# Router logits by a grouped product with a late selector, and another order from the second group's marks to the first gathered rows

## The chip, the cores and the metric

The kernel runs on one core of one Trainium2 chip. The metric is the device time of one execution in microseconds; the median of three runs before the change is 969.06 us (968.68 to 971.01). Engines are named as the profile names them: PE is TensorE (PEld its weight loads), DVE is VectorE, ACT is ScalarE, POOL is GpSimd, SP is the engine that issues most DMAs.

## What is computed

Three layers in a row, all in float32:

```python
# 1. attention: 4 batches, 8 heads, 576 tokens, 64 wide, window of 64 keys
scores = scale * np.matmul(q, k.transpose(0, 1, 3, 2))   # masked outside the window
attn = softmax(scores)
x = np.matmul(attn, v)                                   # -> [2304, 512]
# 2. noisy top-2 router over 8 experts, each 512 -> 1024 -> 512
logits = x @ w_gate
noise_scale = np.log1p(np.exp(x @ w_noise))
noisy_logits = logits + noise_scale * noise
# the two largest per token, softmax over the two
out[mask] += top2_w[mask, k, None] * (np.maximum(x[mask] @ w1[e], 0.0) @ w2[e])
# 3. a dense layer 512 -> 2048 -> 512 with a piecewise quadratic gate
```

The router chooses by the values of the logits, so these are computed in full float32.

## The kernel before, in words

The 2304 tokens are 18 tiles of 128. The attention stage is a pipeline of half-tile steps `u` (0 to 36, `step`, L674); an even step and the odd one after it handle one tile. Everything is issued in program order, and each engine runs its own instructions in that order, so a wait of one instruction holds all behind it on its engine. In an even step stand the scores of the next tile (`A`, L347, products at L355 and L364), the transposes of a finished tile of x (`Ex`, L417: four transposes at L421, a copy by ScalarE at L423), the transposes of a block of probabilities (`C`, L387, copy L389), the row maxima (`top`, L371 on VectorE, scaled on GpSimd at L373) and the exponentials (`soft`, L380 on ScalarE). `Dm` (L392) multiplies by v (L401), normalises on VectorE (L406, L407, L409), issues the store of the tile of x to DRAM (`x_dram`, L412) and moves half a tile of v for the next tile (L414, on GpSimd). Weight chunks for the experts are split into a high and a low part meanwhile (L161 on ScalarE, L162 on VectorE).

The logits of tile i come from `Gm` (L434) in an odd step: four accumulated products (L439; float32 takes two passes each, so eight in the trace) with the transposed tile as weights (128 columns) and 16 columns of router weights moving, into a PSUM bank from a rota of two (`rot`), and a copy to SBUF by VectorE (L442). `wg` in DRAM holds 32 columns a block, of which 16 are zeros.

Tiles are routed in three groups of six (`GROUPS`). When the sixth tile of a group has its logits, `logits` (L667) starts the generator `route` (L488): a chain of small VectorE operations with two ScalarE functions (L500 to L524), the two largest (L528, L531), one-hot rows (L541), their positions by matmuls (L556 to L560), and then twelve marks, two per tile. A mark is a one-hot row on VectorE (`ohr`, L584) and a step row (`ohe`, on VectorE at L591 for odd tiles, on ScalarE at L594 for even ones); its matmul (`place`, L626, at L632) adds it to a table of row numbers in bank 7. `advance` runs the generator in each step, with at most `MARKS` marks: 2 in steps up to 26, 4 from step 27 on; 4 (`TAIL`) behind the attention stage.

When all 24 marks of the first two groups are placed, `early` (L717) runs `finish_ids` (copy of the table L459, four small operations L472 to L475 that give `src_i`) and issues three gathers of rows on GpSimd (L726) for expert 0's first three blocks. `bump` (L606) then corrects the count of expert 0. `xpose` (L739) transposes a gathered block (L748), copies its high part by ScalarE (L751) and its low part by VectorE (L752). The last steps do it like this:

```python
    for u in range(NU + 1):
        step(u)
        ...
        for b in range((0, 1, NA)[max(u - NU + 2, 0)]):
            if ("0a", b) in gat:
                xpose("0a", b, P, Sb[b])
```

The expert stage follows: per chunk a first-layer product (`mm1`, L869; ReLU and split into `h0a` at L877 and L880), and a second-layer product (`mm2`, L935). The logits of the last two tiles, the transposes of the last tile and the third group's chain run in `tail` (L772), a generator of which the loop over the chunks takes one step twice per chunk of expert 0 (`more`):

```python
    def tail():
        logits(NT - 2, NU + 1)
        Ex(NT - 1, NU + 1)
        advance(TAIL)
        yield
        logits(NT - 1, NU + 1)
        while live or oq or pq:
            place()
            advance(TAIL)
            yield
```

## Time and profile before

| | |
|---|---|
| median of 3 runs | 969.06 us |
| profiled execution, its own time | 969.4 us |
| its span, first to last instruction | 967.7 us |
| TensorE busy | 98% of the span |
| VectorE, ScalarE, GpSimd busy | 68%, 46%, 23% |
| mean granted TensorE clock | 0.993 of full speed |

The profile is one execution. Its page gives busy times and groups; the trace behind it can be asked for windows (busy time of each engine in a stretch, with the granted clock), for a timeline in order of time, and for waits (who stood, and what ended it). Times in a timeline are microseconds from the start of the span. Operations that overlap in the pipeline of one engine are merged with their like, so the distance from one start to the next is the better price of a short operation. A releaser in brackets is inferred from semaphores, and where several were waited for it can be another one.

### The profile page before, as it was taken

To read this page: it belongs to the slowest core of one execution; us is meant where nothing else is said; L and a number is where in the kernel's file an instruction comes from. 1 tells how busy PE (TensorE), PEld (TensorE's weight loads), DVE (VectorE), ACT (ScalarE), POOL (GpSimd) and SP (SyncE) were. 2 spreads that over 40 slices of the span, in tenths; PEclk is the share of its full clock that TensorE was granted. 3 is DMA by queue.
4 is the path that set the end of the run, shared out by engine and by line. 5 is a ranking of instruction groups with operands and counts; after the bars stand their busy time and mean duration, and the time that the engine had idled before them with its cause. 6 is when DMAs were issued, how large, how long until landed. Compare 5 with 4: busy or idle time off the path is not lost. (4 is left out here: it accounts for less than half of the span.)

```text
span 967.7 us, 18329 instructions
## 1 busy us (share of the span) xinstructions
PE 944.2 (98%) x6918; PEld 837.0 (86%) x6918; DVE 660.7 (68%) x1377; ACT 446.8 (46%) x921; POOL 218.6 (23%) x269
## 2 busy tenths in 40 slices
PE   8998899999999999999999999999999999999997
PEld 6887789998898988889888888888999899899996
DVE  4689375578997968798442366666766777677664
ACT  6887224356555555555332366344325334442221
POOL 3221113244535434344301020013002201300000
PEclk9999799999999999999999999999999999999999
DMA  8875116557877976967837357584576558556521
GB/s 249 294 236 177 56 45 204 209 195 254 285 253 261 288 250 215 298 218 238 331 118 273 119 197 244 195 302 138 175 261 213 173 174 305 174 164 209 187 95 44
DMA packets 92797, 201.17 MB, mean 208 GB/s; under 512 B 7433, under 2 KB 17929, under 8 KB 92705
## 3 DMA queue, kind: packets, MB, share of 16 engines
q1 hardware_dynamic: 85264, 177.84, 55.4%
q0 software_dynamic: 6144, 19.76, 5.7%
q10 hardware_dynamic: 1296, 2.36, 0.6%
q8 instruction: 55, 0.90, 0.4%
q14 instruction: 38, 0.30, 0.1%
HBM read 159.65 MB, written 40.29 MB: 207 GB/s over the span
## 5 line engine op out<-in xcount | busy, mean ns | idle before, releaser
L935 PE MATMUL bank<-wo,hg 128*128 128x512 f32 x864 | 238.2, 394 | 0.0
L935 PE MATMUL bank<-w,he 128*128 128x512 f32 (+3 forms) x696 | 170.5, 396 | 0.0
L935 PEld LDWEIGHTS bank<-wo,hg 128*128 128x128 f32 x864 | 147.0, 189 | 17.3
L935 PEld LDWEIGHTS bank<-w,he 128*128 128x128 f32 (+3 forms) x696 | 124.7, 184 | 26.7
L869 PE MATMUL bank<-xhie,w 128*128 128x288 f32 (+4 forms) x768 | 120.9, 299 | 1.6 <-DVE he L880 1.5
L869 PEld LDWEIGHTS bank<-xhie,w 128*128 128x128 f32 x768 | 112.0, 188 | 8.6 <-DVE he L880 3.5
L877 ACT ACTIVATE he<-bank 128x288 fp32r<-128x288 f32 (+4 forms) x96 | 40.2, 419 | 149.7 <-PE bank L869 146.1
L162 DVE TENSOR_TENSOR w<-raw,w 128x1024 fp32r<-128x1024 f32 (+1 forms) x71 | 82.0, 1154 | 32.8 <-ACT w L161 32.1
L1188 PEld LDWEIGHTS bank<-xb,wi 128*128 128x128 f32 x576 | 81.6, 191 | 12.2 <-ACT r L887 1.7
L1188 PE MATMUL bank<-xb,wi 128*128 128x256 f32 x576 | 85.9, 285 | 2.4 <-ACT r L887 1.4
L1212 ACT ACTIVATE hg<-cg 128x512 fp32r<-128x512 f32 x64 | 40.3, 629 | 100.5 <-DVE cg L1210 100.5
L1188 PEld LDWEIGHTS bank<-xc,wi 128*128 128x128 f32 x480 | 67.2, 188 | 7.6 <-DVE wg L1173 0.6
L1048 POOL TENSOR_TENSOR y<-y,y 128x512 f32<-128x512 f32 x14 | 19.1, 1362 | 228.2 <-ACT y L1047 228.2
L1188 PE MATMUL bank<-xc,wi 128*128 128x256 f32 x480 | 70.2, 281 | 0.2
L161 ACT ACTIVATE w<-raw 128x1024 fp32r<-128x1024 f32 (+1 forms) x71 | 69.3, 977 | 0.0
L869 PE MATMUL bank<-xloe,w 128*128 128x288 f32 (+4 forms) x384 | 68.1, 299 | 0.0
L880 DVE SCALAR_TENSOR_TENSOR he<-bank,he 128x320 fp32r<-128x320 f32 (+8 forms) x120 | 43.2, 399 | 34.0 <-ACT he L877 33.9
L207 POOL TENSOR_TENSOR td<-rawd 128x512 f32<-128x512 f32 x32 | 33.3, 1040 | 133.5 <-DVE rawd L205 73.7
L1206 ACT ACTIVATE mg<-cg 128x512 f32<-128x512 f32 x64 | 40.0, 626 | 48.6 <-DVE cg L1178 46.9
L1207 DVE SCALAR_TENSOR_TENSOR cg<-mg,cg 128x512 f32<-128x512 f32 x64 | 46.9, 733 | 18.8 <-ACT mg L1206 18.8
L869 PEld LDWEIGHTS bank<-xloe,w 128*128 128x128 f32 x384 | 57.4, 188 | 0.0
L1216 DVE SCALAR_TENSOR_TENSOR hg<-cg,hg 128x512 fp32r<-128x512 f32 x64 | 45.9, 717 | 9.1 <-ACT hg L1212 8.7
(301 smaller groups left out, 1587.0 us busy)
## 6 DMA issues: line engine op xcount, KB each, us to landing
wi<-w1o SPq DMA_DIRECT2D x56, 1024.0 KB, 5.5
raw<-wcat SPq DMA_DIRECT2D x64, 512.0 KB, 5.5
rawd<-wd SPq DMA_DIRECT2D x32, 512.0 KB, 5.0
w1o<-so SPq DMA_DIRECT2D x64, 256.0 KB, 5.7
y<-y_dram SPq DMA_DIRECT2D x30, 256.0 KB, 5.4
vE<-v SPq DMA_DIRECT2D x18, 260.0 KB, 4.7
x_dram<-x SPq DMA_DIRECT2D x18, 256.0 KB, 2.3
k<-kT SPq DMA_DIRECT2D x8, 512.0 KB, 6.6
```

Source lines behind the costliest of these rows:

```text
L161: nc.scalar.activation(w[:, 0, c], t[:, c], AF.Copy)
L162: nc.vector.tensor_tensor(out=w[:, 1, c], in0=t[:, c], in1=w[:, 0, c].bitcast(F32), op=ALU.subtract)
L207: nc.gpsimd.tensor_tensor(out=t, in0=hf, in1=lf, op=ALU.add)
L869: nc.tensor.matmul(ps, lhsT=l[k], rhs=r[:, k, s:s + w], start=(c == 0), stop=(c == len(prods) - 1))
L877: nc.scalar.activation(hh, ps, AF.Relu)
L880: nc.vector.scalar_tensor_tensor(out=t, in0=ps[:, c], scalar=0.0, in1=hh[:, c].bitcast(F32), op0=ALU.max, op1=ALU.subtract)
L935: nc.tensor.matmul(M2[b][0:w], lhsT=h2[:, o:o + w], rhs=r[n], start=(first and a == 0), stop=(last and a == end))
L1188: nc.tensor.matmul(ps, lhsT=w[:, l, k * P:k * P + P], rhs=r[:, m, k, :], start=(c == 0), stop=(c == len(prods) - 1))
L1206: nc.scalar.activation(st["m"], c, AF.Relu, scale=0.5)
L1207: nc.vector.scalar_tensor_tensor(out=c, in0=st["m"], scalar=1.0, in1=c, op0=ALU.min, op1=ALU.subtract)
L1212: nc.scalar.activation(h2[:, 0:T], c, AF.Copy, scale=-1.0)
L1216: nc.vector.scalar_tensor_tensor(out=h2[:, T:2 * T], in0=c, scalar=-1.0, in1=h2[:, 0:T].bitcast(F32), op0=ALU.mult, op1=ALU.subtract)
```

## The change

For fourteen tiles (0 to 10 and 12 to 14) the logits come in two parts. `fold` takes the four 32-column blocks of router weights as weights and moves the transposed tile through them, 128 columns each; the four partial sums go to four groups of 32 partitions of one bank, each by a product of its own, and are copied to SBUF (`lt`; VectorE for tiles 0 to 6, ScalarE for the others). One step later `unfold` multiplies that block, as weights, with a selector `sel` of four stacked unit matrices, which adds the four partial sums and turns them to token order, into a free part of the bank behind the value products. Tiles 11, 15, 16 and 17 keep the product of before. The rest: six marks a step instead of four from step 27 on; the copy of the table reads 4 columns per half first and the others after `src_i`; the last half tile of v is moved by ScalarE instead of GpSimd; the logits of tiles 16 and 17 and the transposes of tile 17 stand ahead of the expert stage, between the transposes of the gathered blocks, and no longer in `tail`.

```diff
--- before.py
+++ after.py
@@ -38,9 +38,10 @@
 GROUPS = [6, 6, 6]
 EARLY = 2
 NA = 3
-MARKS, TAIL = (2, 4), 4
+MARKS, TAIL = (2, 6), 4
 Y0, LOOK = 3, 1
 PTB = 3
+FOLD = 15
 EW, L0, LS, F0 = 7, 1, 4, 1
 SC, WS, HT = 10, 4, 256
 G2 = [2, 4, 4, 4, 4]
@@ -411,7 +412,10 @@
         xs[i] = x
         nc.sync.dma_start(out=x_dram[P * i:P * i + P, :], in_=x.rearrange("p h d -> p (h d)"))
         if i + 1 < NT:
-            nc.gpsimd.tensor_copy(vE[i][0:64, :], vE[i + 1][0:64, :])
+            if i + 2 < NT:
+                nc.gpsimd.tensor_copy(vE[i][0:64, :], vE[i + 1][0:64, :])
+            else:
+                nc.scalar.activation(vE[i][0:64, :], vE[i + 1][0:64, :], AF.Copy)
             vO[i + 1] = vE[i]
 
     def Ex(i, u):
@@ -431,15 +435,44 @@
             tile_group[s + t] = (g, t)
 
 
+    folded = {}
+    sel = ac.tile([P, 2 * E], F32, name="sel")
+    nc.gpsimd.tensor_tensor(out=sel, in0=idn[:, 0:2 * E], in1=idn[:, 32:32 + 2 * E], op=ALU.add)
+    for c in (64, 96):
+        nc.gpsimd.tensor_tensor(out=sel, in0=sel, in1=idn[:, c:c + 2 * E], op=ALU.add)
+
+    def fold(i, u):
+        xt, bk = xts.pop(i), rot(u)
+        for k in range(4):
+            nc.tensor.matmul(bk[32 * k:32 * k + 32, 0:P], lhsT=wg_sb[:, k, :], rhs=xt[:, k, :], start=True, stop=True)
+        lt = wk.tile([P, P], F32, tag="lt", name=f"lt{i}")
+        if i < FOLD // 2:
+            nc.vector.tensor_copy(lt, bk[:, 0:P])
+        else:
+            nc.scalar.activation(lt, bk[:, 0:P], AF.Copy)
+        folded[i] = lt
+
+    def unfold(i):
+        lg = OB[:, 1, LGO:LGO + 2 * E]
+        nc.tensor.matmul(lg, lhsT=folded.pop(i), rhs=sel, start=True, stop=True)
+        keep_logits(i, lg)
+
+    def keep_logits(i, lg):
+        g, t = tile_group[i]
+        if t == 0:
+            lgs_g[g] = gp.tile([P, max(GROUPS), 2 * E], F32, tag="lgs", name=f"lgs{g}", bufs=3)
+        nc.vector.tensor_copy(lgs_g[g][:, t, :], lg)
+        if t == GROUPS[g] - 1:
+            live.append(route(g))
+            next(live[-1])
+
     def Gm(i, u):
         g, t = tile_group[i]
         xt = xts.pop(i)
         lg = (rot(u) if u <= NU else bank[0])[:, LGO:LGO + 2 * E]
         for k in range(4):
             nc.tensor.matmul(lg, lhsT=xt[:, k, :], rhs=wg_sb[:, k, 0:2 * E], start=(k == 0), stop=(k == 3))
-        if t == 0:
-            lgs_g[g] = gp.tile([P, max(GROUPS), 2 * E], F32, tag="lgs", name=f"lgs{g}", bufs=3)
-        nc.vector.tensor_copy(lgs_g[g][:, t, :], lg)
+        keep_logits(i, lg)
 
 
     state = {"C": zero8, "late": False, "first": False}
@@ -456,7 +489,7 @@
             f1 = wk.tile([P, 512], F32, tag="pt", name="f1", bufs=PTB)
             f2 = wk.tile([P, 512], F32, tag="pt", name="f2", bufs=PTB)
         else:
-            nc.vector.tensor_copy(first, IDS2)
+            nc.vector.tensor_copy(first[:, :, 0:NA + 1], IDS2[:, :, 0:NA + 1])
             few = gp.tile([P, 4, NA], F32, tag="few", name="few", bufs=1)
         if dst:
             cum = f1[:, 0:2 * NK].rearrange("p (c j) -> p c j", c=2)
@@ -475,6 +508,7 @@
             nc.vector.scalar_tensor_tensor(out=src_i[:, cl], in0=sm[:, cl], scalar=float(MID), in1=ps[:, cl],
                                            op0=ALU.add, op1=ALU.subtract)
         if not dst:
+            nc.vector.tensor_copy(first[:, :, NA + 1:], IDS2[:, :, NA + 1:])
             return
         nc.vector.tensor_scalar(out=v1, in0=v1, scalar1=0.0, scalar2=float(N), op0=ALU.not_equal, op1=ALU.mult)
         nc.vector.scalar_tensor_tensor(out=sm, in0=sm, scalar=0.0, in1=spare, op0=ALU.is_equal, op1=ALU.mult)
@@ -664,12 +698,8 @@
         soft(u)
     warm(4)
 
-    def logits(i, u):
-        Gm(i, u)
-        g, t = tile_group[i]
-        if t == GROUPS[g] - 1:
-            live.append(route(g))
-            next(live[-1])
+    def direct(i):
+        return i >= FOLD or tile_group[i][0] == EARLY - 1 and tile_group[i][1] == GROUPS[EARLY - 1] - 1
 
     def step(u):
         for c in range(EW):
@@ -698,7 +728,9 @@
             soft(u + 2)
 
         if u % 2 == 1 and 0 <= m - 2 < NT:
-            logits(m - 2, u)
+            (Gm if direct(m - 2) else fold)(m - 2, u)
+        if u % 2 == 0 and 0 <= m - 3 < NT and not direct(m - 3):
+            unfold(m - 3)
         place()
         early()
         advance(MARKS[u > NU - 10])
@@ -755,11 +787,13 @@
         step(u)
         if u == NU - 1:
             xT["0a"] = (wide_x("xhi0a"), wide_x("xlo0a"))
-        for b in range((0, 1, NA)[max(u - NU + 2, 0)]):
-            if ("0a", b) in gat:
-                xpose("0a", b, P, Sb[b])
     assert state["first"]
-
+    Gm(NT - 2, NU)
+    xpose("0a", 0, P, Sb[0])
+    Ex(NT - 1, NU)
+    xpose("0a", 1, P, Sb[1])
+    Gm(NT - 1, NU)
+    xpose("0a", 2, P, Sb[2])
 
     att.close()
     psf = ffn.enter_context(tc.tile_pool(name="psf", bufs=1, space=PS, reuse_waits="tile"))
@@ -770,11 +804,6 @@
     pool["w7"] = w7.enter_context(tc.tile_pool(name="w7", bufs=1, reuse_waits="tile"))
 
     def tail():
-        logits(NT - 2, NU + 1)
-        Ex(NT - 1, NU + 1)
-        advance(TAIL)
-        yield
-        logits(NT - 1, NU + 1)
         while live or oq or pq:
             place()
             advance(TAIL)
```

VectorE at the end of the second group's marks. `ohr1_5_1` is the row of the second group's tile 5 (tile 11 of all), `x15` the normalised tile 15, `first` the copied table, `src_i` the row numbers for the gathers. Before:

```order
L584 TENSOR_SCALAR ohr1_5_0_1986<-io145_179,rf1_1851,tcode2_184 128x128
L591 TENSOR_SCALAR ohe1_5_0_1988<-io145_179,rf1_1851 128x145
L584 TENSOR_SCALAR ohr1_5_1_1990<-io145_179,rf1_1851,tcode2_184 128x128
L591 TENSOR_SCALAR ohe1_5_1_1992<-io145_179,rf1_1851 128x145
L459 COPY first_206<-bank7_78 128x290
L472 TENSOR_TENSOR few_2011<-first_206 128x6
L473 TENSOR_TENSOR few_2011<-few_2011 128x3
L474 TENSOR_SCALAR few_2011<-few_2011 128x3
L475 SCALAR_TENSOR_TENSOR src_i_190<-few_2011 128x3
```

Now:

```order
L618 TENSOR_SCALAR ohr1_5_1_1992<-io145_179,rf1_1892,tcode2_184 128x128
L625 TENSOR_SCALAR ohe1_5_1_1994<-io145_179,rf1_1892 128x145
L407 TENSOR_SCALAR rl15_2012<-ob_106 128x8
L408 RECIPROCAL rl15_2012<-rl15_2012 128x8
L410 TENSOR_TENSOR x15_2015<-ob_106,rl15_2012 128x512
L492 COPY first_210<-bank7_78 128x2x4
L505 TENSOR_TENSOR few_2043<-first_210 128x6
L506 TENSOR_TENSOR few_2043<-few_2043 128x3
L507 TENSOR_SCALAR few_2043<-few_2043 128x3
L508 SCALAR_TENSOR_TENSOR src_i_190<-few_2043 128x3
L511 COPY first_210<-bank7_78 128x2x141
```

Tile 15's three operations stood ahead of the last four marks and stand behind all of them now; the copy is split in two, and its wide part stands behind the row numbers.

TensorE from the end of the attention stage to the first expert products. `xg0a` are the gathered blocks, `xt16` and `xt17` transposed tiles, `w0` and `w1` the first chunks. Before:

```order
L748 MATMUL bank1_74<-idr_170,xg0a_1_2018 128x128 x4
L748 MATMUL bank2_75<-idr_170,xg0a_2_2020 128x128 x4
L869 MATMUL bank1_74<-xhi0a_2057,w0_462 128x384 x8
L869 MATMUL bank1_74<-xlo0a_2058,w0_462 128x384 x4
L439 MATMUL bank0_73<-wg_sb_128,xt16_2069 128x16 x4
L421 MATMUL bank6_2119<-idn_164,x17_2096 128x128 x4
L869 MATMUL bank2_75<-xhi0a_2057,w1_646 128x384 x8
L869 MATMUL bank2_75<-xlo0a_2058,w1_646 128x384 x4
L439 MATMUL bank0_73<-wg_sb_128,xt17_2153 128x16 x4
L935 MATMUL bank3_76<-w0_462,h0a_0_2129 128x512 x3
```

Now:

```order
L474 MATMUL bank3_76<-wg_sb_128,xt16_2116 128x16 x4
L780 MATMUL bank0_73<-idr_170,xg0a_0_2049 128x128 x4
L425 MATMUL bank5_77<-idn_164,x17_2137 128x128 x4
L780 MATMUL bank1_74<-idr_170,xg0a_1_2051 128x128 x4
L474 MATMUL bank3_76<-wg_sb_128,xt17_2155 128x16 x4
L780 MATMUL bank2_75<-idr_170,xg0a_2_2053 128x128 x4
L898 MATMUL bank1_74<-xhi0a_2110,w0_466 128x384 x8
L898 MATMUL bank1_74<-xlo0a_2111,w0_466 128x384 x4
L898 MATMUL bank2_75<-xhi0a_2110,w1_656 128x384 x8
```

The logits of tiles 16 and 17 and the transposes of tile 17 stood between the expert products; now they stand between the transposes of the gathered blocks.

TensorE in the expert stage, at the third group's first marks (`ohr2_0_0`); `h0a_2` is the operand of the third second-layer product. Before:

```order
L935 MATMUL bank3_76<-w2_829,h0a_2_2203 128x512 x3
L935 MATMUL bank4_2118<-w2_829,h0a_2_2203 128x512 x3
L935 MATMUL bank5_77<-w2_829,h0a_2_2203 128x512 x3
L869 MATMUL bank1_74<-xhi0a_2057,w4_1238 128x384 x8
L869 MATMUL bank1_74<-xlo0a_2058,w4_1238 128x384 x4
L657 LDWEIGHTS wz_107
L657 MATMUL bank7_78<-wz_107 128x290
L632 LDWEIGHTS ohr2_0_0_2295
L632 MATMUL bank7_78<-ohe2_0_0_2297,ohr2_0_0_2295 128x145
```

Now:

```order
L898 MATMUL bank2_75<-xhi0a_2110,w3_1042 128x384 x8
L898 MATMUL bank2_75<-xlo0a_2111,w3_1042 128x384 x4
L964 MATMUL bank3_76<-w2_845,h0a_2_2263 128x512 x3
L964 MATMUL bank4_2181<-w2_845,h0a_2_2263 128x512 x3
L964 MATMUL bank5_77<-w2_845,h0a_2_2263 128x512 x3
L691 LDWEIGHTS wz_107
L691 MATMUL bank7_78<-wz_107 128x290
L666 LDWEIGHTS ohr2_0_0_2333
L666 MATMUL bank7_78<-ohe2_0_0_2335,ohr2_0_0_2333 128x145
```

The marks stood behind the first-layer product with `w4`; now they stand one place earlier, behind the second-layer product with `w2`.

## Rows read from the trace of the kernel before

**Rows 1.** The page's part 1: busy time, share of the span and instructions of TensorE.
```profile
PE 944.2 (98%) x6918; PEld 837.0 (86%) x6918; DVE 660.7 (68%) x1377; ACT 446.8 (46%) x921; POOL 218.6 (23%) x269
```

**Rows 2.** Windows of two tiles each, and the gap (columns in the header row).
```profile
core 0: us, PE busy (x) PEld busy (x) DVE busy (x) ACT busy (x) POOL busy (x), PEclk, DMA share, GB/s
35.52:45.02 9.50, 9.50 (x178) 8.62 (x178) 6.13 (x15) 8.42 (x26) 2.38 (x8) 1.00 0.85 287
76.68:88.11 11.43, 9.96 (x184) 8.74 (x184) 10.87 (x48) 9.26 (x29) 2.12 (x6) 1.00 0.61 209
99.40:108.50 9.10, 4.74 (x48) 4.12 (x49) 3.26 (x11) 2.30 (x4) 2.77 (x4) 0.60 0.41 123
```

**Rows 3.** Timeline, TensorE's weight loads of one tile: start us, us, engine, line, operation.
```profile
40.36 0.99 PEld L364 LDWEIGHTS bank<-k,qbuf 64*64 64x64 f32 x32
41.52 0.42 PEld L421 LDWEIGHTS bank<-idn,x 128*128 128x128 f32 x4 [0.17 <-issue]
41.91 0.47 PEld L387 LDWEIGHTS bank<-idn,p 128*128 128x128 f32 x4
42.54 1.01 PEld L401 LDWEIGHTS ob<-vE,pt 128*64 128x64 f32 x32 [0.17 <-issue]
...
44.02 0.97 PEld L439 LDWEIGHTS bank<-wg_sb,xt 128*128 128x128 f32 x8
45.02 0.11 PEld L355 LDWEIGHTS <-id 64*64 64x64 bf16 x3
```

**Rows 4.** Timeline, ScalarE in the same tile (in brackets idle before, releaser).
```profile
41.47 0.71 ACT L161 ACTIVATE w<-raw 128x512 fp32r<-128x512 f32 x1
...
43.92 1.14 ACT L380 ACTIVATE p<-bank,nb 128x128 f32<-128x128 f32 x4 [0.62 <-POOL nb L373]
```

**Rows 5.** Timeline, VectorE, from the second group's middle marks to the first row numbers.
```profile
92.58 1.06 DVE L584 TENSOR_SCALAR ohr<-io,rf,tcode 128x128 f16<-128x128 f16 x3
...
94.12 0.15 DVE L406 TENSOR_SCALAR rl<-ob 128x8 f32<-128x8 f32 x1
...
95.24 0.76 DVE L584 TENSOR_SCALAR ohr<-io,rf,tcode 128x128 f16<-128x128 f16 x3
...
96.88 0.46 DVE L459 COPY first<-bank 128x290 f32<-128x290 f32 x1 [0.32 <-PE bank L632]
...
97.97 0.16 DVE L475 SCALAR_TENSOR_TENSOR src_i<-few 128x3 int32<-128x3 f32 x1
```

**Rows 6.** Timeline, GpSimd's gathers and TensorE up to the second expert product.
```profile
98.43 1.21 POOL L726 DMA_INDIRECT xg0a<-x_dram,src_i  x1 [4.84 <-DVE rl L406]
...
101.21 0.95 POOL L726 DMA_INDIRECT xg0a<-x_dram,src_i  x1 [0.30 <-issue]
102.16 0.62 POOL L414 COPY vE<-vE 64x520 f32<-64x520 f32 x1
...
102.78 0.75 PE L748 MATMUL bank<-idr,xg0a 128*128 128x128 f32 x4 [3.46 <-DMA xg0a<-x_dram,src_i]
...
108.52 2.90 PE L869 MATMUL bank<-xhi0a,w 128*128 128x384 f32 x8 [1.00 <-DVE xlo0a L752]
...
116.22 2.33 PE L935 MATMUL bank<-w,h0a 128*128 128x512 f32 x9
```

**Rows 7.** Windows, two microseconds in the gap (columns as in rows 2).
```profile
102.00:104.00 2.00, 1.22 (x8) 1.23 (x8) 0.00 (x0) 0.43 (x1) 0.78 (x2) 0.50 0.84 252
```

**Rows 8.** Timeline, third group's first marks in the expert stage, VectorE and TensorE.
```profile
124.98 2.29 PE L935 MATMUL bank<-w,h0a 128*128 128x512 f32 x9
...
125.41 0.56 DVE L880 SCALAR_TENSOR_TENSOR h0a<-bank,h0a 128x384 fp32r<-128x384 f32 x1 [0.18 <-ACT h0a L877]
...
127.11 1.57 PE L869 MATMUL bank<-xhi0a,w 128*128 128x384 f32 x8
...
128.14 0.26 DVE L591 TENSOR_SCALAR ohe<-io,rf 128x145 f16<-128x145 f16 x1
...
129.22 0.30 PE L657 MATMUL bank<-wz 128*128 128x290 bf16 x1
```

## Prediction

> **What bounds the kernel now.** I read the busy times first: TensorE is busy for 944.2 of 967.7 us [rows 1], so only work on TensorE, or a wait of TensorE, can move the end. The windows then show where it is not full. A window of two tiles early in the attention stage has TensorE busy for all of its 9.50 us; one late in that stage has 9.96 us of TensorE in 11.43, and VectorE, which marks the tokens there, is busy for 10.87; and the stretch from 99.40 to 108.50 holds only 4.74 us of TensorE, at a mean granted clock of 0.60 [rows 2]. That last stretch is the wait for the first gathered rows: TensorE stands for 3.46 us before it transposes them at 102.78 [rows 6], and in the window around it the clock is 0.50, the 1.2 GHz level [rows 7]; before that it had done nothing for more than two microseconds. The first expert product starts at 108.52 and the second layer's at 116.22 [rows 6]. After that TensorE hardly waits, so what is gained or lost up to there stays to the end.
>
> **The logit product (fourteen tiles).** Today eight passes with a full token block as weights take from 44.02 to 45.02, 1.0 us [rows 3]. The fold runs eight passes with 32 columns of weights and 128 moving columns, in four column groups; the unfold adds two passes whose weight load is as wide as today's, 0.97 / 8 = 0.12 each [rows 3], so 0.24. No row shows a pass of 32 columns. The nearest are the scores, 32 passes of 64 by 64 in 41.52 - 40.36 = 1.16 us, and the value products with all 128 rows and half the columns, 32 in about 1.1 (42.54 to 44.02 less a block of four transposes, 41.91 - 41.52 = 0.39) [rows 3]: 0.035 us a pass, which two or four groups can only reach side by side. At 0.035 the fold costs 0.28; with nothing side by side a pass costs what a transpose does, 0.39 / 4 = 0.10, and the fold 0.8; a weight load that hides behind nothing would add up to 0.12 to each. I take 0.3, nearest to the value products, which use all rows as the fold does: 0.54 instead of 1.0, 0.46 saved a tile, and a total of 6.4 if TensorE bound everywhere.
>
> Here the Trainium skill speaks against the change: "TensorE: Matmul & The Clock Gate", Part 3 on packing small matmuls, says that a weight load runs beside matmuls in flight only if it goes to another row group. The fold's four products use all rows, so by that rule its loads would not hide. Rows 3 show 32 loads of all 128 rows in 1.01 us with their matmuls beside them, which the rule does not give; by it the result would be that of the slow rival below.
>
> What of it lies on the path: in the early window ScalarE is busy for 8.42 of 9.50 us [rows 2], and it also stands for 0.62 because its softmax waits for VectorE, which waited for ScalarE's half of a weight split at 41.47 [rows 4]. 8.42 + 0.62 = 9.04 is what a window can shrink to, 0.46 for two tiles, half of TensorE's saving. Seven tiles lie there: 1.6 us. Their copies out of PSUM (128 columns, on VectorE; between 0.16 for 3 columns and 0.46 for 290 [rows 5]) fit in VectorE's 3.4 us of idle time per window [rows 2]. Later VectorE holds 10.87 of 11.43 [rows 2], and it gets no lighter: the first group's marks start one step later because its last logits do, and two of them now run into the second group's chain. The copies lie on ScalarE there, 1.14 / 4 = 0.29 each [rows 4], with 9.26 of 11.43 busy [rows 2]. I take 0.3 for the rest of the stage. **Term 1: 1.9 saved**, ends 0 and 6.4. The three adds that make the selector run on GpSimd, busy for 2.38 of 9.50 us [rows 2], long before the first unfold: nothing.
>
> **From the marks to the first rows.** Six marks per step instead of four put the last matmul of the second group one step earlier, but all twelve marks still stand on VectorE ahead of the row numbers, now before tile 15's normalisation instead of around it. Four marks take 94.12 - 92.58 = 1.54 and tile 15's three operations 95.24 - 94.12 = 1.12 [rows 5]. So, on the trace's clock, tile 15 starts at 94.12 + 1.54 = 95.7 and is done at 96.8; TensorE, which needs it for its transpose, waits from about 93.6 but for six small mark products. The first copy reads 8 columns instead of 290 (0.3 less than its 0.46), so the row numbers come 1.25 - 0.3 = 0.95 later, at 97.75, against 98.13 now (97.97 + 0.16) [rows 5]. That is only 0.4 earlier. From there to the first transpose takes 102.78 - 98.13 = 4.65, and the gathers follow each other by (101.21 - 98.43) / 2 = 1.4 [rows 6]: rows at 102.4, 103.8 and 105.2.
>
> The larger part is what stands in the wait. From 96.8 TensorE now has, with four transposes 0.4, a value block 1.1, a logit product 1.0 [rows 3]: transposes of tile 15 and one probability block, unfold, value block, transposes, logits of 15, transposes of 16, value block, logits of 16, which is 0.4 + 0.4 + 0.24 + 1.1 + 0.4 + 1.0 + 0.4 + 1.1 + 1.0 = 6.0, to 102.85. Then first gathered block 0.4 and tile 17's transposes 0.4, to 103.65; ScalarE's two copies (0.7 each by 128x512 [rows 4]) let logits of 17 begin at 104.8 and end at 105.8; the third gathered block, its rows in at 105.2, ends at 106.2, and with one more copy the first expert product starts at 107.1. The copy of v rows that GpSimd made behind its gathers, at 102.16 [rows 6], moves to ScalarE between two probability blocks, before the value block at 100.75 needs it: nothing, as ScalarE has under half of this stretch to do; without that cover it is 0.6. VectorE's wide copy of the marks now stands between the row numbers and tile 16; tile 16 is done at 98.95 + 1.1 = 100.05, before TensorE asks at 100.35.
>
> TensorE is not idle long enough here for a drop like today's, so I count both first products at full clock, 129.22 - 127.11 = 2.11 each [rows 8], with no logits between them: second layer at 107.1 + 4.2 = 111.3 instead of 116.22. **Term 2: 4.9 saved.**
>
> **What is late next.** The third group's chain now starts before the expert stage, and its work is taken one unit earlier. Its first four marks stand on TensorE right behind a second-layer product, not behind the next first-layer product. In the trace VectorE ends the unit's operand at 125.41 + 0.56 = 125.97 and the four marks at 128.40, which is 3.4 after that second-layer product began at 124.98; the product lasts until 127.11, 2.1 [rows 8]. TensorE, in order, would stand 1.3 us, and 0.4 at the last four marks (0.43 + 0.56 + 1.54 - 2.13). The position product ahead and the row numbers behind get some 0.3 each. **Term 3: 2.3 lost**, ends 0 and 3.5.
>
> **Sum.** 1.9 + 4.9 - 2.3 = 4.5 saved from the profiled execution's 969.4 (span 967.7 and 1.7 around it), which is 0.3 over the median 969.06; from the median: 964.6.
>
> **The rivals.**
> - The attention stage gives nothing: ScalarE or VectorE takes up the 1.6 as well (for: 8.42 of 9.50 and 10.87 of 11.43 [rows 2]; against: TensorE has no gap at all in the early window). 969.06 - 4.9 + 2.3 = 966.4. Chance 0.20.
> - It gives most and the expert stage waits less: term 1 near 4.5 with 0.3 a tile also late. 969.06 - 4.5 - 4.9 + 2.3 = 962.0. For: VectorE's load is the same in sum and starts earlier. Chance 0.15.
> - The clock falls all the same, in the new wait of TensorE for the last six marks (93.6 to 96.8). For: it fell today after a stand of similar length. Against: small mark products lie in this one. Price: at the 0.50 of rows 7 half of the next 8.6 us (today 102.78 to about 111.4) is lost, 4.3, less some 2 that the list above waits anyway: 967. Chance 0.10.
> - Slower: the fold's passes do not overlap. At 0.10 for the columns and 0.12 for the load the ten passes cost 8 x 0.22 + 0.24 = 2.0, 1.0 more a tile; seven early tiles pay in full, the others have 1.47 of TensorE's idle time per two tiles [rows 2]: 14 - 5.1 = 8.9 lost, against 4.9 - 2.3 = 2.6 gained: 975.4. It decides from 0.16 us a pass on. Rows 3 speak against it. Chance 0.08.
> - The forecast keeps 0.45, and 0.02 is for what I do not see.
>
> **How the numbers follow.** A difference of 0.3%, 2.9 us, is what a measurement of this kernel can tell from none; the border is 966.15. The forecast lies below it nearly whole, the second rival whole, and a small part of the first: 0.64 faster. The clock rival, most of the first, and the forecast's edge are the same: 0.26. Slower: 0.10. The range leaves out the slow rival and the far end of the second: 961.0 to 968.5.
>
> **What would show it.** Right: fold passes near 0.035 us and about 0.5 us for both parts; early windows of two tiles near 9.0; row numbers only about 2.3 us earlier than 98.13 on the changed trace's clock; no wait of 3 us before the gathered rows, and a clock of 1.0 between 95 and 110; TensorE waiting 1 to 1.5 us for marks in the expert stage. Wrong: a clock of 0.50 in that stretch, tile windows as long as before, or a first expert product later than 106.

## The result, and the profile of the changed kernel

The change makes the kernel slower: 983.08 us (median of 6 runs) against 970.12 for the kernel before (6 runs), ratio 1.0126 (95% interval 1.0104 to 1.0148). In a later comparison, on one chip, it is 977.5 against 966.1, ratio 1.0123 (1.0093 to 1.0153). The forecast was 964.6 us, with a chance of 0.64 for faster. The first profiled execution took 985.67 us, its span is 984.0.

The page's part 1 answers to [rows 1]: TensorE is busy for as long as before, and that is 96% of a longer span instead of 98%.

```profile
PE 943.7 (96%) x6946; PEld 831.0 (84%) x6946; DVE 661.4 (67%) x1385; ACT 449.9 (46%) x929; POOL 218.7 (22%) x271
```

Windows answer to [rows 2]: two tiles early, two tiles late, the stretch around the gathered rows, and the first expert product (columns: us, busy time of each engine with instructions, granted clock, DMA share, GB/s).

```profile
39.48:50.78 11.30, 9.13 (x184) 7.58 (x180) 6.43 (x17) 8.58 (x25) 2.45 (x7) 1.00 0.69 223
78.70:90.04 11.34, 9.65 (x189) 8.17 (x188) 9.09 (x31) 9.52 (x30) 2.11 (x6) 1.00 0.82 278
109.30:118.40 9.10, 6.77 (x78) 6.14 (x78) 5.04 (x16) 4.10 (x7) 1.13 (x2) 0.96 0.46 138
118.00:121.00 3.00, 3.00 (x10) 3.00 (x11) 0.44 (x1) 0.00 (x0) 0.00 (x0) 0.50 0.00 0
```

An early pair of tiles takes 11.30 us instead of 9.50, and no engine is full in it, so TensorE waits for something. Its waits say for what (engine, tile and line that waited, the releaser, us in total, times, longest):

```profile
PE ob L402 <- DVE lgs L464: 11.6, 11, 2.0
PE ob L402 <- DVE ixf L568: 2.5, 1, 2.5
...
PE ob L402 <- DVE w L551: 1.8, 1, 1.8
...
PE ob L402 <- DVE ix L565: 0.5, 1, 0.5
```

TensorE stands 16.4 us ahead of the value products (L402, formerly L401): 11.6 for VectorE's copy of the logits (L464), the rest put down to operations of the router chain that stand right beside that copy on VectorE. The kernel before has no such wait in its list. The timelines of two tiles that follow each other show the order (start us, us, engine, line, in brackets the idle time before and its releaser):

```profile
40.90 1.29 DVE L372 TENSOR_REDUCE mx<-bank 128x4 f32<-128x512 f32 x2 [0.92 <-PE bank L365]
42.10 0.16 DVE L464 COPY lgs<-ob 128x16 f32<-128x16 f32 x1
42.41 1.39 PE L402 MATMUL ob<-vE,pt 128*64 128x65 f32 x32 [0.49 <-DVE lgs L464]
...
46.38 0.60 PE L388 MATMUL bank<-idn,p 128*128 128x128 f32 x4
46.67 0.69 DVE L163 TENSOR_TENSOR w<-raw,w 128x512 fp32r<-128x512 f32 x1 [0.90 <-ACT w L162]
46.71 0.30 PEld L457 LDWEIGHTS ob<-sel,lt 128*128 128x128 f32 x2
46.82 0.29 PE L457 MATMUL ob<-sel,lt 128*128 128x16 f32 x2
47.28 1.28 DVE L372 TENSOR_REDUCE mx<-bank 128x4 f32<-128x512 f32 x2
48.48 0.16 DVE L464 COPY lgs<-ob 128x16 f32<-128x16 f32 x1
48.79 1.15 PE L402 MATMUL ob<-vE,pt 128*64 128x65 f32 x32 [1.68 <-DVE lgs L464]
```

In the second tile the selector product is done at 47.1. Its logits lie in the value products' bank, columns 272 to 287; the value products write columns 0 to 259 of it. They wait for the copy all the same, 1.68 us here, and the copy stands on VectorE behind the two row maxima of the step. The Trainium skill, "PSUM — Partial Sum Buffer", section "PSUM bank collisions raise a hardware error", says that the compiler's scheduler makes any two instructions of different engines that touch the same bank and quadrant depend on each other; by that rule disjoint columns do not help, and the trace agrees.

The maxima are only a part of it. In the first of the two tiles they begin as soon as the scores are there, and TensorE stands 0.49 us. In the second they stand behind VectorE's half of a weight split (L163), which had itself waited 0.90 us for ScalarE's half. Such a split stands ahead of seven of the fourteen copies, and these seven make 12.7 of the 16.4 us (1.3 to 2.5 each); the other seven make 3.7 (0.25 to 1.1 each).

The fold itself costs about what was forecast (timeline, weight loads and products of one fold and the next operation's load):

```profile
39.13 0.16 PEld L447 LDWEIGHTS bank<-xt,wg_sb 128*32 128x32 f32 x8 [0.17 <-issue]
39.13 0.43 PE L447 MATMUL bank<-xt,wg_sb 128*32 128x128 f32 x8
39.48 0.11 PEld L356 LDWEIGHTS <-id 64*64 64x64 bf16 x4 [0.20 <-issue]
```

From its start to the next operation's it takes 0.35 us; the unfold's weight loads take 0.30. Together that is 0.65 us where 0.54 were forecast, so a tile saves 0.35 of its 1.0 us and not 0.46.

By stretch, on one chip (profiles b0_before and b1_after; windows from tile 3's scores to tile 17's, from the row numbers to the second layer, from there to the next expert), before and after:

```profile
16.90:89.00 72.10, 69.12 (x1263) 61.06 (x1266) 57.09 (x188) 62.50 (x182) 17.04 (x49) 1.00 0.73 245
98.94:117.58 18.64, 14.07 (x106) 13.37 (x106) 5.60 (x18) 4.47 (x8) 3.75 (x4) 0.73 0.23 72
117.58:173.20 55.62, 54.72 (x333) 48.53 (x333) 37.77 (x129) 19.57 (x39) 10.49 (x10) 1.00 0.36 116
```

```profile
16.30:98.90 82.60, 66.21 (x1283) 54.49 (x1282) 58.07 (x196) 64.17 (x187) 17.02 (x49) 0.98 0.66 216
107.43:121.67 14.24, 12.86 (x145) 12.04 (x143) 6.65 (x22) 6.05 (x12) 3.11 (x3) 1.00 0.36 112
121.67:178.90 57.23, 55.15 (x333) 48.55 (x333) 37.41 (x126) 19.64 (x39) 10.52 (x10) 1.00 0.35 113
```

| stretch | before | after | difference | forecast |
|---|---|---|---|---|
| tile 3's scores to the row numbers | 82.04 | 91.13 | +9.1 | -2.3 (1.9 and 0.4) |
| row numbers to second layer | 18.64 | 14.24 | -4.4 | -4.5 |
| second layer to next expert | 55.62 | 57.23 | +1.6 | +2.3 |
| from there to the end | 793.5 | 793.5 | 0 | 0 |

The first row has the wrong sign. The other two come near the forecast in size; in the second the clock was at 0.73 before and held at 1.00 after, and run 6 will show how much of the 4.4 that is. In the first profile of the change it did not hold (0.50 from 118 to 121).

The table explains these two executions, which differ by 5.8 us (968.37 and 974.19), while the medians differ by 11.4. The mean granted clock of every execution is on record: b0's is 0.993, below the 0.996 that is the median of the 19 other runs there, and its time lies 2.3 us above their median; b1's is 0.998, above the 0.991 to 0.994 of the other three runs of the change, and its time lies 3.3 below its median. So the pair understates the loss, and where the slower executions of the change lose the rest is not seen, since they have no trace.

### The profile page after: what moved, and what is told of

The parts are those of the page before. It is cut to its first block, busy times and chain, and to the rows that moved or that the text cites. A ratio compares the mean times of both kernels' runs of the same rounds, so it can differ in the third digit from the quotient of the medians.

```text
span 984.0 us, 18414 instructions
## 1 busy us (share of the span) xinstructions
PE 943.7 (96%) x6946; PEld 831.0 (84%) x6946; DVE 661.4 (67%) x1385; ACT 449.9 (46%) x929; POOL 218.7 (22%) x271
## 4 chain that ended last, share of the span: by engine, by line
PE 76%; DVE 9%; issue 7%; ACT 5%; DMA 1%; POOL 0%; another core or an unknown queue 0%; SPq 0%; POOLq 0%; DVEq 0%; ACTq 0%
PE bank L964 35%; PE bank L898 18%; PE bank L1217 15%; PE ob L402 2%; DVE mx L372 1%; PE bank L780 1%; PE bank L388 1%; ACT p L381 1%; PE bank L365 1%; ACT w L162 1%; DMA y<-y_dram 1%; PE bank L1275 1%; ACT pt L390 1%; DMA w1o<-so 1%; PE bank L425 0%
## 5 line engine op out<-in xcount | busy, mean ns | idle before, releaser
L163 DVE TENSOR_TENSOR w<-raw,w 128x1024 fp32r<-128x1024 f32 (+1 forms) x71 | 82.2, 1158 | 29.9 <-ACT w L162 26.2
```

The costliest lines, as they stand in the source:

```text
L163: nc.vector.tensor_tensor(out=w[:, 1, c], in0=t[:, c], in1=w[:, 0, c].bitcast(F32), op=ALU.subtract)
```

## The experiments

Tiles are the program's here. The expectations count the score products from tile 1 on, so that their "first scores", "tile 2", "tile 10" and "tile 16" are tiles 1, 3, 11 and 17. The runs were made on five chips, and each chip has its own runs of the kernel before: 975.55 us (1 to 4), 966.1 (b0, b1, 8, 5), 966.01 (9, 10, 6, 7), 972.3 (11, 12), 966.5 (13 to 15). Ratios are therefore to these runs. The expectations of runs 1 to 4 are in microseconds for a kernel before of 970; as ratios their 967 is 0.997, their 978 is 1.008 and their 982 is 1.012. The theory: the logits' copy makes the next user of its bank wait. The rivals: the copies overload VectorE and ScalarE (B), or the loss is elsewhere in the change (C).

**1. The logits in a score bank.**

```diff
-        lg = OB[:, 1, LGO:LGO + 2 * E]
+        lg = Sb[(u + 1) % 3][:, 0:2 * E]
```

(`u` is passed to `unfold`.)

> The changed kernel with one thing moved: the selector product writes its logits into the score bank that is free in that step, not behind the value products in their bank. Same instructions, same order on each engine. Theory A (the value products stand because the copy of the logits out of their bank is queued on VectorE behind the row maxima): the 16.4 us that TensorE stood ahead of the value products fall below 2, a window of two tiles early goes back to 9.5 or less, and the time is 967 us (964 to 970). Rival B (VectorE and ScalarE are late because they got fourteen copies of 128 columns more): the wait moves to another line, the windows stay above 11 us, and the time stays above 978. Rival C (the loss is in the other parts of the change): above 978 as well, with the value products no longer waiting.

Measured: 979.52 us, ratio 1.0052 (1.0029 to 1.0076), between the theory's 0.997 and the rivals' 1.008. The value products wait no longer, and tile 3 to the row numbers falls to 81.4 us (16.03 to 97.45): the wait is where the theory has it. But the stage is only about half a microsecond shorter than before, and an early pair of tiles takes 9.65 to 9.79 us, not 9.5. The scores now stand for the exponentials (1.9 of the 3.6 us below stand ahead of tile 3, as in the kernel before). The clock (0.80 between 100 and 120) and the third term are the likely rest; the 967 was too low.

```profile
PE bank L356 <- ACT p L381: 3.6, 6, 0.9
```

**2. The selector product ahead of the step's transposes, same bank.**

```diff
+            if 0 <= m - 3 < NT and not direct(m - 3):
+                unfold(m - 3)
             if 0 <= m - 2 < NT:
                 Ex(m - 2, u)
...
-        if u % 2 == 0 and 0 <= m - 3 < NT and not direct(m - 3):
-            unfold(m - 3)
```

> The changed kernel with the selector product (same bank as in the change) issued ahead of the transposes of the step, right behind the scores, so that VectorE copies the logits ahead of the two row maxima. Theory A: the bank may be shared as long as the copy isn't queued behind the maxima: the wait of the value products falls from 16.4 us below 3, time 967 (964 to 970), within 2 of the run with the other bank. If the bank itself were the trouble wherever the copy stands: above 975. Rival B: above 978.

Measured: 981.01 us, ratio 1.0055 (1.0026 to 1.0084). The value products' wait is 3.6 us instead of 16.4 (below 3 was expected), but the selector product itself now waits for the fold's copy and other work (1.8, 0.9, 0.6 and 0.4 us), since it comes a block earlier: 84.1 us up to the row numbers (16.9 to 100.96). The copy's place matters, but at this place the product comes too early for its operand, and the time stays far from the 967.

**3. No fold.**

```diff
-FOLD = 15
+FOLD = 0
```

> All tiles keep the eight-pass logit product of before; the other parts of the change stay (six marks a step, the copy of the table in two pieces, the last v copy on ScalarE, the logits of the last two tiles ahead of the expert stage). Theory A: no wait of the value products, and the attention stage as long as before; by the trace of the changed kernel these parts gain 1.2 us between the row numbers and the second layer (16.9 against 18.1) and lose 1.8 us in the third group's marks, so 969.7 (967 to 972). The forecast's terms 2 and 3 would make it 966.5. Rival C: above 978.

Measured: 979.09 us, ratio 1.0032 (1.0001 to 1.0063): not the 0.8% that rival C's 978 means. Tile 3 to the row numbers takes 80.9 us; but the second layer comes 20.6 us after the row numbers, longer than before, with the clock at half for 14 us:

```profile
97.87:118.48 20.61, 18.12 (x141) 16.89 (x140) 6.70 (x21) 5.98 (x12) 3.10 (x3) 0.67 0.26 78
102.00:116.00 14.00, 12.58 (x79) 11.79 (x80) 4.56 (x14) 3.22 (x6) 0.05 (x1) 0.53 0.23 72
```

Ahead of it TensorE had stood for 0.9 us at 96.3 and for 1.4 at 101.1.

**4. The fold alone on the kernel before.**

Added are `fold`, `unfold` and `direct`, and in `step`:

```diff
-            logits(m - 2, u)
+            (Gm if direct(m - 2) else fold)(m - 2, u)
+        if u % 2 == 0 and 0 <= m - 3 < NT and not direct(m - 3):
+            unfold(m - 3)
```

> The kernel before with the fold and the selector product alone, placed as in the change; marks, copies and the end of the attention stage as before. Theory A: it carries the whole loss, with more than 10 us of waits ahead of the value products: 982 (978 to 986). Rival B: the same time, but the waits would not be put down to the copy of the logits. Rival C: 967 (the forecast's term 1 alone).

Measured: 984.54 us, ratio 1.0092 (1.0058 to 1.0126), 16.2 us of waits ahead of the value products. The fold carries most of the loss: 9.0 us here, where the other parts alone (run 3) lost 3.5 on the same chip.

**b0 and b1. Both kernels on one chip.** In all four runs above, and in the first profile of the changed kernel, TensorE stood for "issue", that is for nothing that the profile shows, ahead of the 64-column products of a late unit of the expert stage, the spill unit (1.7 to 2.3 us). So both kernels were profiled once more.

> The kernel before, once more with a profile, on the chip of the next three runs. In the four experiments so far 6 to 8 us were lost behind the attention stage that its first profile does not show: TensorE stood for 'issue' ahead of the 64-column products of the spill unit (2 us, at half clock) and ahead of a few second-layer products. If these belong to the chip and not to the change, this profile shows them too and its span is near 974; if they belong to the change, it shows none and the span is near 968.

> The changed kernel once more, on the same chip as the run of the kernel before with a profile and as the next two. By the traces it reaches the second layer 7.4 us later than before and the next expert 9.1 later: ratio 1.0095, whatever the chip adds to both. The first comparison gave 1.0126.

Measured: 968.37 us in the one execution, and 977.5, ratio 1.0123 (1.0093 to 1.0153; 1.0095 was expected). Neither profile shows the stands; they came back in 11 and 12, on a chip where the kernel before also takes 972.3. That they go with the chip and not with the change is inferred: run 3 shows them without a fold, and b1 and run 8 show none with it; but on the chips of runs 1 to 4, 11 and 12 the kernel before was not profiled. The ratio of the change is the same in both comparisons.

**8. The logits in the rota's next bank.**

```diff
-        lg = OB[:, 1, LGO:LGO + 2 * E]
+        lg = rot(u)[:, LGO:LGO + 2 * E]
```

(`u` is passed to `unfold`.)

> The changed kernel with the selector product's logits in the next bank of the rota (where the fold and the transposes go), not in the value products' bank and not in a score bank. In the score bank the value products stopped waiting, but the scores then stood 3.6 us for the exponentials and the attention stage was as long as before, not shorter. Theory A (each bank that the logits borrow passes their copy's lateness on to its next user): here the next user is the fold of the next step, 2 us later, so nothing waits; attention as in the kernel before or up to 2 us shorter, no wait of the value products, ratio 1.000 (0.998 to 1.003). Rival B (ScalarE and VectorE have no room for the copies, wherever the logits go): the waits go to the transposes or the scores, attention longer by 1 us or more, ratio 1.004 or above.

Measured: 969.07 us, ratio 1.0024 (1.0005 to 1.0042). The change takes 977.5 on the same chip, so the bank alone gives back 8.4 of the 11.4 us; tile 3 to the row numbers takes 82.3 us (16.24 to 98.50) instead of 91.1. This is the plainest evidence that the shared bank is the cause. That nothing would wait did not come true. The wait has a new name: that bank holds the transposed tile, which ScalarE has yet to copy.

```profile
PE bank L457 <- ACT xt L427: 4.6, 14, 1.0
```

**5. No fold, clock held.** The added products' results are read by nobody.

```diff
+            if u in (NU - 2, NU):
+                warm((4, 6)[u == NU], Sb[u == NU])
             if 0 <= m - 2 < NT:
                 Ex(m - 2, u)
...
     xpose("0a", 2, P, Sb[2])
+    warm(3, Sb[1])
```

> The run without the fold, with thirteen bf16 products of 128 by 512 added whose results nobody reads: four ahead of the transposes of tile 15, six ahead of those of tile 16, three ahead of the first expert product, where TensorE stood 0.9, 1.4 and 0.7 us. Without the fold the granted clock was 0.50 from 102 to 116 on the trace, and the second layer began at 118.5. Theory A (the forecast's order of that stretch was right and its clock wrong): the clock stays at 1.0 there and the second layer begins at 112 to 114, ratio 0.997 against the kernel before. Rival (the stretch waits for ScalarE's copies and the gathers): the second layer stays at 117 or later even at full clock, ratio 1.003.

Measured: 965.89 us, ratio 0.9996 (0.9986 to 1.0007). Over this stretch the trace is as the theory has it: clock 1.00, row numbers to second layer 15.05 us instead of 20.6; the span is 2.7 us shorter than b0's.

```profile
97.68:112.73 15.05, 14.42 (x150) 12.41 (x149) 6.76 (x21) 6.03 (x12) 3.10 (x3) 1.00 0.35 106
```

The median moves by 0.2 only, not by the 0.3% of the theory. The kernel before runs at 964.57 to 970.89 us there, this one at 964.83 to 966.93. The recorded clocks say why the trace promised more: b0 was an execution of the kernel before at a low mean clock (0.993, and 968.37 us), while the median one has 0.996 and 966.1; this version has 0.997 or more in all of its ten. It takes away the slow executions and hardly moves the middle one.

**6. The kernel before, clock held.**

```diff
+        if u == NU - 1:
+            warm(14, Sb[2])
         for b in range((0, 1, NA)[max(u - NU + 2, 0)]):
```

> The kernel before with fourteen products without use in the 3.5 us in which TensorE stands for the first gathered rows. Theory A (half of what the changed order gains there is the clock): it stays at 1.0 after the stand, the value products of tile 17 take 1.15 instead of 2.0 us and the first expert product 2.9 less, so the second layer begins 2.5 to 3.5 us earlier; ratio 0.997. Rival (the stand ends with the gathered rows and ScalarE's copies whatever the clock): under 1 us, ratio 1.000.

Measured: 965.62 us, ratio 0.9996 (0.9985 to 1.0006). On its trace the second layer comes 15.5 us after the row numbers (97.77 to 113.31) instead of 18.64, 3.1 earlier; the median moves by 0.4: the comparison is again with b0 at its low clock. So of the 4.4 us in the table's second row about 3.1 are the clock, and the new order by itself is worth about 1.3 there, or 0.5 in run 5 (15.05 against 15.54).

**9 and 10. The selector product one step later, in the bank of the next fold**; 10 adds the products of run 5.

```diff
+            bk = rot(u)
+            if m - 3 in folded:
+                unfold(m - 3, bk)
+            if direct(m - 2):
+                Gm(m - 2, u, bk)
+            else:
+                fold(m - 2, bk)
```

> The changed kernel with the selector product one step later and its logits in the bank that the next tile's fold (or logit product) takes in that step anyway, in columns of their own: no bank gets a user it did not have, and the fold's copy is two steps old. Theory A (every bank lent to the logits made its next user wait for a copy: 16 us in the value products' bank, 3.6 in the score bank, 4.6 in the rota's next bank): now nothing waits, a tile takes 4.45 to 4.55 us in the early half of the attention stage instead of 4.75, and the stage from the first scores to those of tile 16 takes 78.6 us, 1.9 less than before, as the forecast's term 1 had it; ratio 0.996 to 0.999. Rival B (ScalarE and VectorE have no room for fourteen more copies): a tile takes 4.75 or more, the stage 80.5 or more, ratio 1.000 or above.

> The run before with the thirteen products without use that held the clock at 1.0 in the run without the fold. Theory A: the two gains add: second layer 1.9 earlier than in that run, 110.8 less the shift of the start, ratio 0.995 to 0.998 and the lowest of all. Rival: the clock holds without them, so they change nothing against the run before.

Measured: 981.05 us, ratio 1.0155 (1.0140 to 1.0169), and 979.93, 1.0140 (1.0124 to 1.0156): no better than the change. The fold shares its bank with a copy issued ahead of it, so it waits for that copy:

```profile
PE bank L447 <- DVE lgs L464: 18.2, 12, 3.3
```

The ratio lies on rival B's side, but not by its mechanism: it is the theory's wait at another place, at the same price.

**7. The maxima behind the selector product and its copy.**

```diff
+        if u % 2 == 0 and 0 <= m - 3 < NT and not direct(m - 3):
+            unfold(m - 3)
         if u % 2 == 0 and u + 2 < NU:
             top(u + 2)
...
-        if u % 2 == 0 and 0 <= m - 3 < NT and not direct(m - 3):
-            unfold(m - 3)
```

> The changed kernel with the two row maxima issued behind the selector product and its copy, the product in the value products' bank as in the change. Theory A (the value products wait because the copy stands behind 1.3 us of maxima): their wait falls from 16.4 to below 5 us, but the maxima, and with them the exponentials, start about 1 us later in each tile; ratio 1.004 to 1.009, between the change and the runs with another bank. If the maxima ahead of the copy were not the cause, the wait stays above 12 us and the ratio at 1.012.

Measured: 971.4 us, ratio 1.0058 (1.0043 to 1.0073); the value products' wait is 7.8 us, not under 5. So the place behind the maxima is about half of it. Two early tiles show the rest:

```profile
28.38 1.15 PE L402 MATMUL ob<-vE,pt 128*64 128x65 f32 x32 [0.36 <-DVE lgs L464]
...
33.89 1.15 PE L402 MATMUL ob<-vE,pt 128*64 128x65 f32 x32 [1.03 <-DVE lgs L464]
```

The longer wait has the weight split still ahead of the copy. In the shorter one VectorE had stood idle for 2.00 us and copied the logits at once, and TensorE waited all the same: with the product right ahead of the value products in their bank, some 0.36 us a tile is left even then, about what the fold saves (0.35). Up to the row numbers the stage takes 86.4 us, 4.7 less than in the change and 4.4 more than before; how much of that the later maxima cost was not separated.

**11 and 12. Run 9 with both products ahead of both copies**; 12 adds the products of run 5.

```diff
             bk = rot(u)
-            if m - 3 in folded:
-                unfold(m - 3, bk)
+            then = unfold(m - 3, bk)
...
-                fold(m - 2, bk)
+                fold(m - 2, bk, then)
```

Here `unfold` issues its product alone, and `fold` calls `then` (the copy of the logits) behind its own products.

> As the run with the shared bank, with one change: both products of the step (selector product of the tile before, then the fold) are issued ahead of both copies. In that run the fold stood 18.2 us for the copy of the logits, since its bank was read by a copy that was queued ahead of it on VectorE; that was the same wait at a third place, and a slip of that run's order. Theory A (the fold itself is cheap, the loss is only in who shares a bank with a copy that comes late): no wait ahead of the fold, selector or value products, a tile takes 4.5 us in the early half of the attention stage, the stage 78.6 us, ratio 0.996 to 0.999. Rival B (ScalarE and VectorE have no room for the copies): a tile 4.75 or more, the stage 80.5 or more, and the waits stand ahead of the scores or the transposes; ratio 1.000 to 1.003.

> The run before plus the thirteen products without use of the run without the fold. Theory A: 1.9 us less than that run, 964.0 of span becoming 962; ratio 0.996 to 0.998, lowest of all. Rival B: ratio 0.999 to 1.001, as without the fold.

Measured: 977.54 us, ratio 1.0059 (1.0033 to 1.0085), and 971.92, 1.0004 (0.9985 to 1.0023). No bank's user waits for the logits now. The early tiles take 4.4 and 5.1 us in turn (scores at 35.31, 40.42 and 44.81). In the shorter one VectorE waits 1.07 us for ScalarE's half of a weight split, its row maxima come late by that, and with them the exponentials, for which the scores of the next tile then wait:

```profile
PE bank L356 <- ACT p L381: 3.7, 6, 1.0
...
PE bank L594 <- ACT pt L390: 2.8, 2, 1.7
```

The first line is as in run 1, where the logits lay in a score bank; here no score bank is lent. So those waits belong to the shorter tile and not to the lent bank.

Windows from tile 3's scores to tile 11's and on to tile 17's, run 11 and then b0:

```profile
16.90:54.30 37.40, 36.31 (x719) 29.96 (x718) 25.45 (x61) 32.69 (x96) 8.95 (x27) 1.00 0.78 259
54.30:89.60 35.30, 30.13 (x568) 24.25 (x564) 32.20 (x134) 30.32 (x92) 7.97 (x22) 1.00 0.68 227
```

```profile
16.90:55.30 38.40, 38.33 (x705) 34.21 (x704) 26.79 (x72) 34.16 (x100) 9.73 (x29) 1.00 0.77 256
55.30:89.00 33.70, 30.79 (x559) 26.86 (x563) 30.30 (x117) 28.34 (x84) 7.31 (x21) 1.00 0.69 232
```

The first half gains 1.0 us, the second loses 1.6, with VectorE at 32.2 of 35.3. That speaks for rival B in the rest of the fold: its saving on TensorE meets two engines that leave little room. Run 11's ratio lies above even rival B's 1.003; the clock was 0.80 between the row numbers and the second layer, and 1.00 in run 12.

**13. Fold for tiles 0 to 6 only, as in 12, all seven copies on VectorE.**

```diff
-FOLD = 15
+FOLD = 7
...
-        if i < FOLD // 2:
+        if i < FOLD:
```

> As the run with both products ahead of both copies and the thirteen products without use, but the fold for tiles 0 to 6 only (their copies on VectorE); tiles 7 to 17 have the eight-pass product. In the run with fourteen folds the early half of the attention stage (scores of tile 2 to those of tile 10) took 37.4 instead of 38.4 us, and the rest 35.3 instead of 33.7, with VectorE busy for 32.2 of it. Theory A (the fold pays where VectorE has room and costs where it has none): the first half keeps the 1.0, the second is back at 33.7, ratio 0.996 (0.994 to 0.998). Rival (the second half is late because the first group's chain starts a step later): the second half stays above 35, ratio 0.999 or above.

Measured: 967.06 us, ratio 1.0003 (0.9990 to 1.0017). The first half takes 37.9 us (0.5 gained, not 1.0), the second 34.3: it loses 0.6 though its own tiles are those of before. The first group's chain, whose last logits come a step later, moves VectorE's work into the second half (31.8 us busy there against 30.3 in b0), and that is the likely reason; the rest of run 11's 1.6 would then go with the copies there. Neither was tested alone. The sum is zero.

**14. Run 5 with the third group's chain one unit later.**

```diff
     def tail():
+        yield
         while live or oq or pq:
```

> The run without the fold and with the thirteen products, with the third group's chain one unit later in the expert stage, where it stood in the kernel before. Theory A (term 3: taking the chain one unit earlier put its marks behind a second-layer product and costs TensorE 1.6 us of waits): the stretch from the second layer's start to the next expert falls from 57.2 to 55.8 us, ratio 0.998 (0.996 to 0.9995). Rival (the wait goes to the next gather, whose rows come one unit later): 57 us or more, ratio as without it, 0.9996.

Measured: 964.41 us, ratio 0.9972 (0.9958 to 0.9987). Second layer to next expert:

```profile
113.48:169.02 55.54, 54.64 (x332) 48.44 (x332) 37.66 (x128) 19.99 (x40) 10.54 (x10) 1.00 0.37 117
```

55.5 us against 57.2 in run 5 and in the change, and 55.6 before: the third term is the place of the chain. The waits agree: in that stretch TensorE stood 1.3 us for the operand of a second-layer product and 0.8 for marks in the change, and 0.9 for the operand and nothing for marks here and before. This version is 2.1 us below the kernel before; it has no fold.

**15. Runs 13 and 14 together.**

> Both together: seven folds, the thirteen products without use, the third group's chain one unit later. If both theories hold, the gains add: ratio 0.995 (0.993 to 0.997), the lowest of all runs; if only one does, 0.997.

Measured: 965.79 us, ratio 0.9988 (0.9974 to 1.0002): not lower than 14. The seven folds add nothing.

## Why the prediction was wrong

- **Term 1 (1.9 saved) failed, and with it the sign.** The step is "the unfold adds two passes ..., so 0.24": it priced the selector product on TensorE and the fold's copy as work for which VectorE has idle time, and had no term for what waits for the copy of the logits. The unfold's output lies in "a free part of the bank behind the value products" and is issued right ahead of them, so the copy must end between the two, and on VectorE it stood behind the two maxima (1.28 us) and in every second tile or so behind a weight split too. The prediction had read in rows 4 that VectorE waits there for ScalarE, and charged it to ScalarE's window only. What it cost is 16.4 us of TensorE, 16.4 / 14 = 1.2 a tile. Measured: 9.1 us lost up to the row numbers, where the other parts alone (run 3) gain about 1. Run 8 gives 8.8 of them back by another bank alone.
- **The 1.9 are not there even without that wait.** The fold and the unfold take 0.65 us and not 0.54. In run 12 the stretch up to the row numbers takes 82.0 us (16.73 to 98.75), against 82.04 before and 81.3 in run 5 without the fold: 0.7 lost. Early, a pair takes 37.4 / 4 = 9.35 us in run 11 where ScalarE was to allow 9.04; late, 0.3 saved were taken although VectorE held 10.87 of 11.43 [rows 2], and 1.6 were lost. The first rival's "attention gives nothing" is what runs 8 and 11 to 13 show.
- **Term 2 (4.9) came out near its size, but most of it is the clock.** In b1 the row numbers to the second layer take 14.24 us instead of 18.64; 13.55 were forecast. The order alone is worth 0.3 to 1.3: at a held clock the old order takes 15.54 (run 6), the new one 14.24 to 15.28 (b1, 5, 12 and 15). The rest rests on the sentence that TensorE is not idle long enough for a drop, and that holds only in some executions: the clock of this stretch was 1.00 in b1, 0.90 in the first profile of the change and 0.67 in run 3. The row numbers came 0.8 to 1.1 us earlier without the fold (runs 5 and 3), against 0.4. The clock rival (967, chance 0.10) came true in run 3, and it was priced at 2.4 us where it cost 5.5 (20.6 against 15.05).
- **Term 3 (2.3 lost) was right in its place and too large**: 1.6, and run 14 gives it back. Of the 1.7 us of waits for marks 0.8 came, and 0.4 more for the operand of a second-layer product.
- **The slow rival was wrong in its mechanism.** A fold pass takes 0.044 us (0.35 / 8), far below its 0.16. The rule that stood behind it (the Trainium skill, "TensorE: Matmul & The Clock Gate", Part 3), by which a weight load hides only in another row group, does not fit these rows: eight loads of all 128 rows end 0.16 us after the first began, beside their matmuls. The right sign came from a mechanism that no rival named.

## What to carry to other kernels

Before a result is put into a free corner of a bank, write down who touches that bank next and behind what the reading engine's copy stands: that wait is the price, whatever the product costs. Run 8 shows how to test it: another bank, and nothing else. A saving on the engine that bounds a stage is worth only what the next engine in line leaves, so read the busy time of the second and third engine over the same window first. Where a chain is shortened, see what the pulled-forward work meets: here one `yield` gave back 1.6 us. And before a gain read from a pair of traces is believed, compare the mean clock of the two executions with the other runs of each kernel.

## What was not expected of the hardware

In run 3 TensorE stood for 0.9 and 1.4 us in a stretch of small products; right behind the second stand the granted clock fell to 0.50, the 1.2 GHz level, and it stayed there from about 103 to 116 although TensorE was busy for 12.58 of the 14.0 us from 102 to 116. With thirteen products without use it was 1.00 over the whole stretch in runs 5, 12 and 15, but with the same thirteen products it fell to 0.50 for some 3 us in runs 13 and 14 (0.90 over the stretch). In the changed kernel the stretch ran at full clock in one execution and at half for 3 us in another. So what holds the clock there is not settled by these runs.
